# A planner that treats one PSUM bank as one place and keeps TensorE's tiled groups together

## The chip, the core and the metric

The kernel runs on one core of one Trainium2 chip. The metric is the device time of one execution in microseconds (us). Before the change it is 1250.54 us, the median of three runs that lie between 1249.49 and 1253.12 us.

## What is computed

Attention over 8 batches and 8 heads (576 positions, head size 64) with a threshold on the scores, and after it a feed-forward network (FFN) over all 4608 tokens. All data is float32.

```python
scores = scale * np.matmul(q, k.transpose(0, 1, 3, 2))
thresh = np.max(scores, axis=-1, keepdims=True) - tau
scores = np.where(scores >= thresh, scores, -1000000000.0)
attn = np.exp(scores - max); attn = attn / (attn.sum() + 1e-09)
x = np.matmul(attn, v)            # heads side by side: (4608, 512)
h = x @ w_in                      # (4608, 2048)
g = s * np.maximum(h, 0.0) ** 2 + b
out = g @ w_out                   # (4608, 512)
```

## The kernel before

**Attention** is done in 64 visits. A visit takes two heads of one batch and 256 of their queries; every second visit also takes the 64 last queries (the tail). A visit has four tiles of 128 queries by 576 keys, and one more if it has a tail. For a tile TensorE makes the scores in one of the banks `s0`, `s1` (early on also `o`), DVE scales them and takes the minimum (L395), ACT takes the exponential (L406), DVE applies the threshold and sums (L409), and POOL divides (L413). The first eight visits are turned over by TensorE transposes (L423, L425), the later ones by DVE (L446, L448) and by DMA into `er`. Then TensorE makes a visit's value products (L476) into the bank `pv`.

**The FFN** is done in 18 blocks of 256 tokens. A block has 16 steps, one for each 128 columns of `w_in`, so 288 steps in all. A step has twelve matmuls of 256 columns (L599, in f32 parts) into one half of the bank `h`; the halves `h0` and `h1` take turns. ACT reads that half with a Relu (L606) and squares it (L607), `gh` and `gl` are the two parts of the result (L609, L610), and two triples of matmuls of 512 columns (L616) add the step's share to the bank `o`.

**Groups of matmuls that use only a part of the array** (tiled, in the words of the change) are three: the early scores of two heads side by side (L352, tiles of 64 by 128, 24 groups of 4), the tails' scores in quarters (L374, 64 by 64, 28 groups of 4), and the value products (L476, 128 by 64, 64 groups of 10). All the other matmuls (L363, L599, L616 and some early ones) use 128 by 128. The profile counts twice as many instructions for L352, L374 and L476, since each of these f32 matmuls is two there.

**The order of all work** is made by the class `Plan`. Each piece of work is put in with `add`: its engine, a cost, the names it reads (`r`) and writes (`w`), and a rank `at`. From the names `add` works out what must come first. `ordered` is a list scheduler: it takes the engine that is free first and the ready piece of the lowest rank, forwards and backwards in turn (`run`, 8 rounds for each of 18 settings of slack), and `played` rates each order by playing it with random delays; the best one is emitted. Each engine then runs its instructions in the order emitted. The semaphores are not the planner's: a layer below sets them, from the emitted order and the tiles that instructions use, and there the bank `h` is one tile.

Names of the plan that the change touches: a step's matmuls write `h0` or `h1`, and in addition `hs`, which no piece of work reads (`step`); its Relu reads `h0` or `h1`. `sums` (L563) is one product for the bias, also in bank `h`. `pairs` (in `scores`), `last_rows` and `value_products` give the costs of the three tiled groups.

Of the kernel before, what the change touches and what calls it, by code (L numbers as in the profile page):

```python
# [13 lines left out]
AF = mybir.ActivationFunctionType  # L14
# [11 lines left out]
WEIGHTS_AT, WEIGHTS_EACH = 12, 0.8  # L26
FIRST_WEIGHTS = 4
SECOND = 3.5


class Plan:
    HANDOVER, TO_PE = 50, 150
    PASS, OVER = 100, 400
    SPARE = {"DVE": 100, "ACT": 100, "POOL": 100, "SP": 300}
    SHARES = 0.2, 0.4, 0.7
    LATER = 1.0, 1.2, 1.4
# [4 lines left out]
    def __init__(self):  # L41
        self.ops, self.writer, self.readers = [], {}, {}

    def add(self, engine, cost, emit, r=(), w=(), at=0.0, port=False):
        n, deps = len(self.ops), set()
        for k in r:
            if k in self.writer:
                deps.add(self.writer[k])
        for k in w:
            if k in self.writer:  # L50
                deps.add(self.writer[k])
            deps.update(self.readers.pop(k, ()))
            self.writer[k] = n
        for k in r:
            self.readers.setdefault(k, []).append(n)
        deps.discard(n)
        self.ops.append((engine, cost[0], cost[-1], emit, deps, at, port or engine == "POOL"))

    def run(self):
        ops = self.ops  # L60
# [27 lines left out]
        return sum(self.played(order, *slow) for slow in self.SLOW) / len(self.SLOW)  # L88

    def played(self, order, seed, cold, hand=60, to_pe=150, same=40):  # L90
        ops, free, done, port = self.ops, {}, [0.0] * len(self.ops), 0.0
        late = random.Random(seed)
        for _, n in order:
            e, busy, ready, _, deps, _, shared = ops[n]
            t = free.get(e, 0.0)
            for d in deps:
                if ops[d][0] != e:
                    t = max(t, done[d] + (to_pe if e == "PE" else hand))
                elif e != "PE":
                    t = max(t, done[d] + same)  # L100
            if shared and port > t:
                t = port
            tail = ready - busy
            if e in ("DVE", "ACT", "POOL"):
                busy += late.expovariate(1 / self.DELAY)
            elif e == "PE" and t < self.EARLY:
                busy *= cold
            elif e == "SP":
                tail += late.expovariate(1 / self.LANDING)
            free[e] = t + busy  # L110
            if shared:
                port = t + busy
            done[n] = t + busy + tail
        return max(done) / 1000

    def ordered(self, before, after, rank, busy, done, back):
        ops = self.ops
        left = [len(b) for b in before]
        ready = [0.0] * len(ops)
        free, coming, there = {}, {}, {}  # L120
        for n, o in enumerate(ops):
            free[o[0]] = 0.0
            coming.setdefault(o[0], [])
            there.setdefault(o[0], [])
            if not left[n]:
                heapq.heappush(coming[o[0]], (0.0, n))
        order, port = [], 0.0
        for _ in ops:
            best = None
            for e in free:  # L130
                t = free[e]
                while coming[e] and coming[e][0][0] <= t:
                    n = heapq.heappop(coming[e])[1]
                    heapq.heappush(there[e], (rank[n], n))
                if not there[e]:
                    if not coming[e]:
                        continue
                    t = coming[e][0][0]
                if best is None or t < best[0]:
                    best = t, e  # L140
            t, e = best
            while coming[e] and coming[e][0][0] <= t:
                n = heapq.heappop(coming[e])[1]
                heapq.heappush(there[e], (rank[n], n))
            n = heapq.heappop(there[e])[1]
            if ops[n][6] and port > t + self.PASS:
                for at, m in sorted(there[e]):
                    if not ops[m][6] and busy[m] < port - t + self.OVER:
                        there[e].remove((at, m))
                        heapq.heapify(there[e])  # L150
                        heapq.heappush(there[e], (rank[n], n))
                        n = m
                        break
            if ops[n][6]:
                t = max(t, port)
                port = t + busy[n]
            order.append((t, n))
            free[e] = t + busy[n]
            for u in after[n]:
                if ops[u][0] == e == "PE":  # L160
                    late = busy[n]
                else:
                    late = busy[n] + done[u] - busy[u] if back else done[n]
                    p = n if back else u
                    late += 0 if ops[u][0] == e else self.TO_PE if ops[p][0] == "PE" else self.HANDOVER
                ready[u] = max(ready[u], t + late)
                left[u] -= 1
                if not left[u]:
                    heapq.heappush(coming[ops[u][0]], (ready[u], u))
        order.sort()  # L170
        return order
# [3 lines left out]
def tile_attention_ffn(ctx: ExitStack, tc: tile.TileContext, qT, kT, v, tau, w_in, w_out, s, b, out):  # L175
    nc = tc.nc
# [52 lines left out]

    plan = Plan()  # L230

    def pe(cost, fn, r, w, at):
        plan.add("PE", (cost, cost + 170), fn, r, w, at)

    def dve(cost, fn, r, w, at, port=False):
        plan.add("DVE", cost, fn, r, w, at, port)
# [98 lines left out]
    def scores(vs, i, t):  # L335
        n = vs.n
        if t is None:
            def both():
                for hf in range(2):
                    cs = slice(hf * HS, (hf + 1) * HS)  # L340
                    nc.tensor.matmul(flat["s0"][:, S0 + hf * HS:S0 + (hf + 1) * HS], qd[n], kr[:, n, cs], start=True, stop=True)
            pe(970, both, [("k", n)] + vs.kd, ["s0"], i - SCORES_AHEAD)
            return

        ks = [vs.scores_in(i + j, j) for j in range(2)]

        def pairs():
            for hf in range(2):
                cs = slice(hf * HS, (hf + 1) * HS)
                for j in range(2):  # L350
                    r = slice(j * D, (j + 1) * D)
                    nc.tensor.matmul(flat[ks[j]][:, S0 + hf * HS:S0 + (hf + 1) * HS], qr[r, n, t * P:(t + 1) * P], kr[r, n, cs],  # L352
                                     start=True, stop=True)
        pe(980, pairs, vs.kq + ["guard"] + (["h0"] if not i else []), ks, i - SCORES_AHEAD)

    def split_scores(vs, i, j, t):
        sk, qc = f"s{i % 2}", slice(t * P, (t + 1) * P)
# [9 lines left out]
    def last_rows(vs, i, before):  # L367
        sk = f"s{i % 2}"

        def quarters():  # L370
            for r in range(2):
                rows, cs = slice(r * D, (r + 1) * D), slice(r * HS, (r + 1) * HS)
                for j in range(2):
                    nc.tensor.matmul(flat[sk][j * T:(j + 1) * T, S0 + r * HS:S0 + (r + 1) * HS], qr[rows, j, NB:NB + T],  # L374
                                     kr[rows, j, cs], start=True, stop=True)
        cost, r, w = 860, [(x, o) for x in ("rk", "rq") for o in (0, D)], [sk]
        values = None
        if before is not None:
            more, values, r_, w_ = value_products(before)
# [2 lines left out]
        def both():  # L382
            quarters()
            if values:
                values()
        pe(cost, both, r, w, i - SCORES_AHEAD)

    def tile_of(vs, i, j, t):
        sk = vs.scores_in(i, j)
# [78 lines left out]
    def value_products(vs):  # L468
        n, nb = vs.n, vs.nb
        ps = bank["pv"]  # L470

        def products():
            for c in range(5):
                r = slice(0, T if vs.pe and c == NQ else P)
                for j in range(2):
                    nc.tensor.matmul(ps[j * D:(j + 1) * D, 0:32 * nb], vb[r, n, j, c], er[r, n, j, 0:nb, 32 * c:32 * c + 32],  # L476
                                     start=(c == 0), stop=(c == 4))
        return (250 + 66.6 * 4.33 * nb, products,
                [("v", n, x) for x in range(3)] + [("er", n, j, e) for j in range(2) for e in range(nb)], ["pv"])

    def with_v(vs, at, done=False):
        ps = bank["pv"]
        if not done:
            pe(*value_products(vs), at)
        xk = xs[vs.bi, vs.u]
        act((268, 372), lambda: nc.scalar.copy(out=xb[xk][:, vs.pair], in_=ps[:, 0:NB]), ["pv"],
            [("x", xk, vs.pair)], at)
# [73 lines left out]

    def sums(at):
        pe(900, lambda: nc.tensor.matmul(bank["h"], ones.bitcast(F32), bias_t, start=True, stop=True), ["bias", "ones"],  # L563
           ["h0", "h1", "hs"], at)
        act((480, 620), lambda: nc.scalar.mul(out=bias_t, in_=bank["h"], mul=b_t), ["h0", "h1", "b"], ["bias"], at)

    def xhl():
# [4 lines left out]
    class Block:  # L572
# [16 lines left out]
        def step(self, f, at):  # L589
# [9 lines left out]
                        nc.tensor.matmul(ps, w[:, c, :], x[:, c, :], start=(c == 0 and i == 0), stop=(c == NC - 1 and i == 2))  # L599
            if f in (0, NF - 1):  # L600
                for c in range(0, NC, 2):
                    pe(6 * 120.9, lambda c=c: products(range(c, c + 2)), [("xh", c // 2), ("xl", c // 2), (f"w{f}", "i")], [f"h{k}", "hs"], at)
            else:
                pe(3 * NC * 120.9, lambda: products(range(NC)), [(x, c) for x in ("xh", "xl") for c in range(2)] + [(f"w{f}", "i")],
                   [f"h{k}", "hs"], at)
            act((272, 383), lambda: nc.scalar.activation(out=g, in_=ps, func=AF.Relu), [f"h{k}"], [f"g{k}"], at)  # L606
            act((322, 417), lambda: nc.scalar.activation(out=g, in_=g, func=AF.Square), [f"g{k}"], [f"g{k}"], at)  # L607
            eng, do = (nc.vector, dve2) if self.last else (nc.gpsimd, pool)
            act((302, 405), lambda: nc.scalar.copy(out=hi, in_=g), [f"g{k}"], [f"gh{n}"], at)  # L609
# [218 lines left out]
```

## Time and profile before

| | |
|---|---|
| median of three runs | 1250.54 us (1249.49 to 1253.12) |
| the profiled execution | 1250.1 us, of which its span is 1248.3 us |
| TensorE (PE) busy | 1211.1 us, 97% of the span |
| DVE, ACT, POOL busy | 807.1, 767.5, 719.7 us |
| mean granted TensorE clock | 0.987 |

The span is the time from the first to the last instruction of the program; 1.8 us of the profiled execution lie around it. An engine's busy time is the time in which at least one of its instructions runs, and the ends of matmuls are modelled, so successive matmuls overlap in the rows: the distance from one start to the next is what a matmul costs.

### The profile page before, as it was taken

To read this page: it belongs to the slowest core of one execution; us is meant where nothing else is said; L and a number is where in the kernel's file an instruction comes from. 1 tells how busy PE (TensorE), PEld (TensorE's weight loads), DVE (VectorE), ACT (ScalarE), POOL (GpSimd) and SP (SyncE) were. 2 spreads that over 40 slices of the span, in tenths; PEclk is the share of its full clock that TensorE was granted. 3 is DMA by queue.
4 is the path that set the end of the run, shared out by engine and by line. 5 is a ranking of instruction groups with operands and counts; after the bars stand their busy time and mean duration, and the time that the engine had idled before them with its cause. 6 is when DMAs were issued, how large, how long until landed. Compare 5 with 4: busy or idle time off the path is not lost.

```text
span 1248.3 us, 24523 instructions
## 1 busy us (share of the span) xinstructions
PE 1211.1 (97%) x7926; PEld 990.0 (79%) x7926; DVE 807.1 (65%) x2158; ACT 767.5 (61%) x1890; POOL 719.7 (58%) x822
## 2 busy tenths in 40 slices
PE   7789999999999999999999999999999999999998
PEld 5467778787887888788878888888888888887887
DVE  7987876667767676576666677666766666663011
ACT  5777755666666676565665666566656665653443
POOL 3766845576666775575565666557566656652200
PEclk7889999999999999999999999999999999999999
DMA  7950257678768776667666676566766666652000
GB/s 254 282 184 25 53 140 159 153 169 182 173 157 186 170 172 153 150 144 170 136 160 151 150 173 156 143 147 161 162 142 160 161 157 152 158 134 72 1 17 17
DMA packets 259534, 180.66 MB, mean 145 GB/s; under 512 B 83536, under 2 KB 238160, under 8 KB 259408
## 3 DMA queue, kind: packets, MB, share of 16 engines
q1 hardware_dynamic: 259120, 178.98, 59.0%
q8 instruction: 63, 1.03, 0.3%
q14 instruction: 63, 0.52, 0.1%
q10 hardware_dynamic: 288, 0.13, 0.0%
HBM read 87.03 MB, written 9.44 MB: 77 GB/s over the span
## 4 chain that ended last, share of the span: by engine, by line
PE 91%; DVE 4%; ACT 2%; issue 1%; DMA 1%; POOL 1%; SPq 0%; ACTq 0%; DVEq 0%; POOLq 0%
PE h L599 33%; PE o L616 32%; PE pv L476 12%; PE s L363 9%; PE s L352 2%; PE s L374 1%; DVE s L395 1%; ACT g L606 1%; PE pv L425 1%; DVE tr L409 1%; DMA qr<-in_q_dram 0%; DMA tau_t<-in_tau_dram 0%; DVE em L409 0%; DVE k L549 0%; PE o L352 0%
## 5 line engine op out<-in xcount | busy, mean ns | idle before, releaser
L599 PE MATMUL h<-xh,w 128*128 128x256 f32 x2304 | 466.7, 286 | 11.3 <-ACT g L606 11.0
L599 PEld LDWEIGHTS h<-xh,w 128*128 128x128 f32 x2304 | 376.9, 190 | 38.2 <-ACT g L606 23.5
L616 PE MATMUL o<-w,gh 128*128 128x512 f32 x1152 | 366.8, 400 | 0.8 <-DVE em L636 0.6
L599 PE MATMUL h<-xl,w 128*128 128x256 f32 x1152 | 326.1, 283 | 1.5 <-DVE xl L585 1.4
L610 POOL TENSOR_TENSOR gl<-g,gh 128x256 fp32r<-128x256 f32 x272 | 202.8, 747 | 212.0 <-ACT gh L609 188.2
L395 DVE TENSOR_SCALAR_CACHE_REDUCE s<-s,nsc 128x576 f32<-128x576 f32 x283 | 230.5, 819 | 143.1 <-PE s L363 120.8
L413 POOL TENSOR_SCALAR em<-em,st,zero 128x576 f32<-128x576 f32 x270 | 230.1, 853 | 156.7 <-DVE st L412 102.2
L409 DVE SCALAR_TENSOR_TENSOR em<-s,st,em 128x577 f32<-128x577 f32 x268 | 217.5, 812 | 105.8 <-ACT st L404 67.9
L406 ACT ACTIVATE em<-s,st 128x576 f32<-128x576 f32 x268 | 197.8, 738 | 95.9 <-DVE s L395 62.4
L616 PEld LDWEIGHTS o<-w,gh 128*128 128x128 f32 x1152 | 197.0, 189 | 46.3 <-issue 20.4
L616 PE MATMUL o<-w,gl 128*128 128x512 f32 x576 | 225.1, 391 | 0.0
L599 PEld LDWEIGHTS h<-xl,w 128*128 128x128 f32 x1152 | 219.7, 191 | 6.1 <-DVE xl L585 2.0
L446 DVE STREAM_TRANSPOSE tr<-em 128x512 f32<-128x512 f32 x252 | 178.2, 707 | 56.9 <-POOL em L413 47.3
L606 ACT ACTIVATE g<-h 128x256 f32<-128x256 f32 x288 | 109.2, 380 | 171.0 <-PE h L599 160.6
L328 POOL TENSOR_TENSOR k<-kr,k 64x576 fp32r<-64x576 f32 x104 | 148.5, 1428 | 54.1 <-ACT k L327 40.2
L476 PE MATMUL pv<-er,vb 128*64 128x256 f32 (+1 forms) x1280 | 172.8, 416 | 1.6 <-ACT er L434 1.6
L609 ACT CAST gh<-g 128x256 fp32r<-128x256 f32 x288 | 116.2, 405 | 56.6 <-PE o L616 52.9
L363 PE MATMUL s<-k 128*128 128x288 f32 x832 | 144.1, 297 | 0.6 <-POOL k L328 0.6
L363 PEld LDWEIGHTS s<-k 128*128 128x128 f32 x832 | 127.7, 188 | 19.7 <-issue 4.9
L476 PEld LDWEIGHTS pv<-er,vb 128*64 128x64 f32 x1280 | 86.4, 138 | 70.5 <-issue 12.9
L616 PEld LDWEIGHTS o<-w,gl 128*128 128x128 f32 x576 | 108.4, 188 | 24.5
L607 ACT ACTIVATE g<-g 128x256 f32<-128x256 f32 x288 | 119.9, 417 | 5.7
(104 smaller groups left out, 953.3 us busy)
## 6 DMA issues: line engine op xcount, KB each, us to landing
er<-tr SPq DMA_DIRECT2D x448, 160.0 KB, 3.3
kr<-in_k_dram SPq DMA_DIRECT2D x116, 288.0 KB, 4.2
vb<-in_v_dram SPq DMA_DIRECT2D x128, 128.0 KB, 2.8
qr<-in_q_dram SPq DMA_DIRECT2D x56, 160.0 KB, 4.4
er<-tr SPq DMA_DIRECT2D x112, 80.0 KB, 2.5
w<-in_moe_w_in_dram SPq DMA_DIRECT2D x16, 512.0 KB, 6.6
w<-in_moe_w_out_dram SPq DMA_DIRECT2D x16, 512.0 KB, 5.7
out_dram<-oo SPq DMA_DIRECT2D x30, 256.0 KB, 2.6
```

Source lines behind the costliest of these rows:

```text
L328: pool((1500, 1500), lambda: nc.gpsimd.tensor_tensor(out=z()[D:P], in0=kr[D:P, j], in1=z()[D:P].bitcast(F32), op=ALU.subtract), rk + [("z" ...
L363: nc.tensor.matmul(flat[sk][:, S0 + hf * HS:S0 + (hf + 1) * HS], lazy["q"][:, x, j, qc], lazy["k"][:, j, cs], start=(x == 0), stop=(x == 1))
L395: dve((740, 875), lambda: nc.vector.tensor_scalar(out=ps[:, S0:S0 + S], in0=ps[:, S0:S0 + S], scalar1=nsc, scalar2=None, op0=ALU.mult, op1 ...
L406: act((632, 740), lambda: nc.scalar.activation(out=ev, in_=ps[:, S0:S0 + S], func=AF.Exp, bias=st8[:, 0:1], scale=-1.0), [sk, (ks_, 0)], [ ...
L409: dve((742, 830), lambda: nc.vector.scalar_tensor_tensor(out=eb, in0=ps[:, S0:S0 + S + 1], scalar=st8[:, 1:2], in1=eb, op0=ALU.is_le, op1= ...
L413: pool((795, 825), lambda: nc.gpsimd.tensor_scalar(out=ev, in0=ev, scalar1=st8[:, 4:5], scalar2=zero, op0=ALU.mult, op1=ALU.add), [em_k, ( ...
L446: nc.vector.transpose(out=to[:, :, 0:NQ].rearrange("p m c q -> p m (c q)"), in_=ev[:, 0:M].rearrange("p (m r) -> p m r", m=4))
L476: nc.tensor.matmul(ps[j * D:(j + 1) * D, 0:32 * nb], vb[r, n, j, c], er[r, n, j, 0:nb, 32 * c:32 * c + 32], start=(c == 0), stop=(c == 4))
L599: nc.tensor.matmul(ps, w[:, c, :], x[:, c, :], start=(c == 0 and i == 0), stop=(c == NC - 1 and i == 2))
L606: act((272, 383), lambda: nc.scalar.activation(out=g, in_=ps, func=AF.Relu), [f"h{k}"], [f"g{k}"], at)
L610: do((712, 740), lambda: eng.tensor_tensor(out=lo, in0=g, in1=hi.bitcast(F32), op=ALU.subtract), [f"g{k}", f"gh{n}"], [f"gl{n}"], at)
L616: nc.tensor.matmul(bank["o"][:, t, :], a[:, ts_], w, start=(f == 0 and i == 0), stop=(f == NF - 1 and i == 2))
```

## The change

The bank `h` becomes one place in the plan: every step writes both `h0` and `h1`, and its Relu reads both, so that in the plan no step may start before the Relu of the step ahead of it is done. The name `hs` goes. Then the plan knows which PE groups are tiled. When a PE group differs in that from the one before, the plan adds `TURN` = 95 ns, in `ordered` and in `played`; one tiled shape after another counts as no change. When the last PE group was tiled and the next by rank is not, `ordered` looks among the ready groups for a tiled one whose rank is less than `NEAR` = 8000 ns later, and takes that first. The costs of tiled groups become: pairs 1170 instead of 980, quarters 650 instead of 860, value products 170 + 267 for each 32 columns instead of 250 + 288.4. The matmuls and all other instructions stay the same in kind and number.

```diff
+PAIR = 1170
...
+    TURN, NEAR = 95, 8000
...
-        self.ops.append((engine, cost[0], cost[-1], emit, deps, at, port or engine == "POOL"))
+        self.ops.append((engine, cost[0], cost[-1], emit, deps, at, port or engine == "POOL", tiled))
...
     def played(self, order, seed, cold, hand=60, to_pe=150, same=40):
...
             t = free.get(e, 0.0)
+            if e == "PE":
+                t += self.TURN * (tiled != mode)
+                mode = tiled
...
             n = heapq.heappop(there[e])[1]
+            if e == "PE" and mode and not ops[n][7]:
+                for at, m in sorted(there[e]):
+                    if ops[m][7] and at < rank[n] + self.NEAR:
+                        there[e].remove((at, m))
+                        heapq.heapify(there[e])
+                        heapq.heappush(there[e], (rank[n], n))
+                        n = m
+                        break
+            if e == "PE":
+                t += self.TURN * (mode != ops[n][7])
+                mode = ops[n][7]
...
-        pe(980, pairs, vs.kq + ["guard"] + (["h0"] if not i else []), ks, i - SCORES_AHEAD)
+        pe(PAIR, pairs, vs.kq + ["guard"] + (["h0"] if not i else []), ks, i - SCORES_AHEAD, True)
...
-        cost, r, w = 860, [(x, o) for x in ("rk", "rq") for o in (0, D)], [sk]
+        cost, r, w = 650, [(x, o) for x in ("rk", "rq") for o in (0, D)], [sk]
...
-        pe(cost, both, r, w, i - SCORES_AHEAD)
+        pe(cost, both, r, w, i - SCORES_AHEAD, True)
...
-        return (250 + 66.6 * 4.33 * nb, products,
+        return (170 + 267 * nb, products,
...
-            pe(*value_products(vs), at)
+            pe(*value_products(vs), at, True)
...
-           ["h0", "h1", "hs"], at)
+           ["h0", "h1"], at)
...
-                   [f"h{k}", "hs"], at)
-            act((272, 383), lambda: nc.scalar.activation(out=g, in_=ps, func=AF.Relu), [f"h{k}"], [f"g{k}"], at)
+                   ["h0", "h1"], at)
+            act((272, 383), lambda: nc.scalar.activation(out=g, in_=ps, func=AF.Relu), ["h0", "h1"], [f"g{k}"], at)
```

What this does to the emitted order is seen at three places. Lines of the changed kernel are 16 higher: L599 is L615 there, L616 is L632, L363 is L379, L476 is L492, L374 is L390. Left of the arrow stands the tile written, right of it the tiles read; `w4_489` before and `w4_486` in the change are both the weights of step 4 of a block. A line of "..." leaves out a step's other matmuls.

PE, where one block of the FFN begins (its steps 4 to 6). Before:

```order
L363 MATMUL s1_99<-k_1521 128x288 x4
L599 MATMUL h_102<-xh_609,w4_489 128x256
...
L599 MATMUL h_102<-xh_609,w5_562 128x256
...
L599 MATMUL h_102<-xh_609,w6_621 128x256
...
L476 MATMUL pv_101<-er_84,vb_83 64x256 x10
L616 MATMUL o_100<-w0_268,gh2_94 128x512 x2
```

The same place in the change:

```order
L492 MATMUL pv_101<-er_84,vb_83 64x256 x10
L615 MATMUL h_102<-xh_597,w4_486 128x256
...
L379 MATMUL s1_99<-k_1509 128x288 x4
L379 MATMUL s0_98<-k_1509 128x288 x4
L615 MATMUL h_102<-xh_597,w5_545 128x256
...
L632 MATMUL o_100<-w0_248,gh2_94 128x512 x2
```

Before, three steps followed each other; now two groups of scores stand between steps 4 and 5, and second products (L632) after step 5. In the whole program a step followed the step before it with nothing between 39 times before, and does so 2 times now; with one group of scores (L363) alone between them 18 times before, 1 time now.

PE, a tail's quarters and the value products near it. Before, the value products:

```order
L599 MATMUL h_102<-xh_609,w1_299 128x256
L476 MATMUL pv_101<-er_84,vb_83 64x320 x10
L363 MATMUL s0_98<-k_1521 128x288 x4
L616 MATMUL o_100<-w14_1351,gh1_93 128x512 x2
```

and the quarters, some 60 rows later:

```order
L616 MATMUL o_100<-w1_299,gl1_96 128x512
L374 MATMUL s0_98<-kr_81,qr_82 64x288 x4
L616 MATMUL o_100<-w1_299,gh1_93 128x512 x2
```

In the change:

```order
L615 MATMUL h_102<-xh_597,w4_486 128x256
L492 MATMUL pv_101<-er_84,vb_83 64x320 x10
L390 MATMUL s0_98<-kr_81,qr_82 64x288 x4
L615 MATMUL h_102<-xh_597,w5_545 128x256
```

The two tiled groups now follow each other. In the whole program tiled groups stand beside each other 25 times, 11 times before, and PE goes from untiled to tiled work or back 182 times, 210 times before.

PE, the first step of the first block. Before:

```order
L425 MATMUL pv_101<-k_87,em0_77 128x128 x4
L599 MATMUL h_102<-xh_609,w0_268 128x256
...
L599 MATMUL h_102<-xh_609,w0_268 128x256
L423 MATMUL s1_99<-k_87,em1_78 64x128
L425 MATMUL pv_101<-k_87,em1_78 128x128 x4
L352 MATMUL s0_98<-kr_81,qr_82 128x288
...
L425 MATMUL pv_101<-k_87,tr0_79 128x128 x4
L599 MATMUL h_102<-xh_609,w0_268 128x256
```

In the change:

```order
L441 MATMUL pv_101<-k_87,em1_78 128x128 x4
L615 MATMUL h_102<-xh_597,w0_248 128x256
...
L615 MATMUL h_102<-xh_597,w0_248 128x256
L357 MATMUL s0_98<-kr_81,k_87 128x288 x2
L615 MATMUL h_102<-xh_597,w1_309 128x256
```

The first step's two halves stood apart, with transposes and scores between them; now they are one run.

## Rows read from the trace of the kernel before

**Rows 1.** The page: PE's busy time, and the granted clock in 40 slices.

```profile
PE 1211.1 (97%) x7926; PEld 990.0 (79%) x7926; DVE 807.1 (65%) x2158; ACT 767.5 (61%) x1890; POOL 719.7 (58%) x822
...
PEclk7889999999999999999999999999999999999999
```

**Rows 2.** The page: the chain that ended last, share of the span by engine.

```profile
PE 91%; DVE 4%; ACT 2%; issue 1%; DMA 1%; POOL 1%; SPq 0%; ACTq 0%; DVEq 0%; POOLq 0%
```

**Rows 3.** Windows: busy us of each engine by stretch.

```profile
core 0: us, PE busy (x) PEld busy (x) DVE busy (x) ACT busy (x) POOL busy (x), PEclk, DMA share, GB/s
0.00:31.00 31.00, 24.20 (x106) 15.95 (x106) 22.55 (x70) 16.60 (x31) 11.16 (x25) 0.78 0.78 253
31.00:62.00 31.00, 23.39 (x132) 14.57 (x134) 30.57 (x80) 23.36 (x49) 23.46 (x19) 0.84 0.91 287
62.00:94.00 32.00, 27.14 (x166) 19.62 (x165) 25.79 (x65) 22.39 (x53) 20.61 (x19) 0.89 0.58 180
...
562.00:625.00 63.00, 62.05 (x416) 52.24 (x412) 39.67 (x107) 38.34 (x97) 36.84 (x44) 1.00 0.67 156
```

**Rows 4.** PE's waits from 94 us on: who waited for whom, us, times, longest.

```profile
PE h L599 <- ACT g L606: 10.5, 20, 1.0
PE h L563 <- ACT g L606: 1.0, 1, 1.0
```

**Rows 5.** Timeline, PE and ACT: the third of three steps in a row begins.

```profile
1031.70 0.28 PE L599 MATMUL h<-xl,w 128*128 128x256 f32 x1
1031.82 0.28 PE L599 MATMUL h<-xh,w 128*128 128x256 f32 x1
1032.19 0.38 ACT L606 ACTIVATE g<-h 128x256 f32<-128x256 f32 x1 [1.92 <-PE h L599]
...
1032.63 0.38 PE L599 MATMUL h<-xh,w 128*128 128x256 f32 x1 [0.53 <-ACT g L606]
```

**Rows 6.** Timeline of PE: one group of scores between untiled groups.

```profile
331.31 0.69 PE L363 MATMUL s<-k 128*128 128x288 f32 x4
331.83 0.63 PE L616 MATMUL o<-w,gh 128*128 128x512 f32 x2
```

**Rows 7.** Timeline of PE: value products alone between two steps.

```profile
577.42 0.28 PE L599 MATMUL h<-xl,w 128*128 128x256 f32 x1
577.54 0.28 PE L599 MATMUL h<-xh,w 128*128 128x256 f32 x1
577.75 2.38 PE L476 MATMUL pv<-er,vb 128*64 128x256 f32 x20
580.06 0.39 PE L599 MATMUL h<-xh,w 128*128 128x256 f32 x1
580.28 0.28 PE L599 MATMUL h<-xl,w 128*128 128x256 f32 x1
```

**Rows 8.** Timeline of PE: a tail's quarters alone.

```profile
639.62 0.72 PE L374 MATMUL s<-kr,qr 64*64 64x288 f32 x8
640.26 0.39 PE L599 MATMUL h<-xh,w 128*128 128x256 f32 x1
```

**Rows 9.** Timeline of PE: value products and quarters side by side.

```profile
335.96 2.38 PE L476 MATMUL pv<-er,vb 128*64 128x256 f32 x20
338.27 0.72 PE L374 MATMUL s<-kr,qr 64*64 64x288 f32 x8
338.92 0.39 PE L599 MATMUL h<-xh,w 128*128 128x256 f32 x1
339.14 0.28 PE L599 MATMUL h<-xl,w 128*128 128x256 f32 x1
```

**Rows 10.** PE's waits before 94 us.

```profile
PE s L352 <- DVE em L409: 4.9, 3, 4.1
PE s L423 <- POOL tr L413: 2.4, 4, 1.1
...
PE h L599 <- DVE xl L585: 1.4, 1, 1.4
...
PE h L599 <- ACT g L606: 0.5, 1, 0.5
```

**Rows 11.** Waits of the other engines over the whole span, and DMA landing.

```profile
ACT g L606 <- PE h L599: 160.6, 141, 5.0
...
DVE s L395 <- PE s L363: 120.8, 120, 4.6
...
er<-tr SPq DMA_DIRECT2D x448, 160.0 KB, 3.3
```

More of the change, by code (lines that the diff above doesn't have):

```diff
@@ L42, in __init__, with add @@
         self.ops, self.writer, self.readers = [], {}, {}
-    def add(self, engine, cost, emit, r=(), w=(), at=0.0, port=False):
+    def add(self, engine, cost, emit, r=(), w=(), at=0.0, port=False, tiled=False):
         n, deps = len(self.ops), set()
@@ L90, in played @@
     def played(self, order, seed, cold, hand=60, to_pe=150, same=40):
-        ops, free, done, port = self.ops, {}, [0.0] * len(self.ops), 0.0
+        ops, free, done, port, mode = self.ops, {}, [0.0] * len(self.ops), 0.0, False
         late = random.Random(seed)
         for _, n in order:
-            e, busy, ready, _, deps, _, shared = ops[n]
+            e, busy, ready, _, deps, _, shared, tiled = ops[n]
             t = free.get(e, 0.0)
+            if e == "PE":
+                t += self.TURN * (tiled != mode)
+                mode = tiled
             for d in deps:
@@ L126, in ordered @@
                 heapq.heappush(coming[o[0]], (0.0, n))
-        order, port = [], 0.0
+        order, port, mode = [], 0.0, False
         for _ in ops:
@@ L230, in tile_attention_ffn, with pe @@
     plan = Plan()
-    def pe(cost, fn, r, w, at):
-        plan.add("PE", (cost, cost + 170), fn, r, w, at)
+    def pe(cost, fn, r, w, at, tiled=False):
+        plan.add("PE", (cost, cost + 170), fn, r, w, at, tiled=tiled)
     def dve(cost, fn, r, w, at, port=False):
@@ L601, in step @@
                 for c in range(0, NC, 2):
-                    pe(6 * 120.9, lambda c=c: products(range(c, c + 2)), [("xh", c // 2), ("xl", c // 2), (f"w{f}", "i")], [f"h{k}", "hs"], at)
+                    pe(6 * 120.9, lambda c=c: products(range(c, c + 2)), [("xh", c // 2), ("xl", c // 2), (f"w{f}", "i")], ["h0", "h1"], at)
             else:
                 pe(3 * NC * 120.9, lambda: products(range(NC)), [(x, c) for x in ("xh", "xl") for c in range(2)] + [(f"w{f}", "i")],
-                   [f"h{k}", "hs"], at)
-            act((272, 383), lambda: nc.scalar.activation(out=g, in_=ps, func=AF.Relu), [f"h{k}"], [f"g{k}"], at)
+                   ["h0", "h1"], at)
+            act((272, 383), lambda: nc.scalar.activation(out=g, in_=ps, func=AF.Relu), ["h0", "h1"], [f"g{k}"], at)
             act((322, 417), lambda: nc.scalar.activation(out=g, in_=g, func=AF.Square), [f"g{k}"], [f"g{k}"], at)
```

## The prediction

> **What bounds the kernel now.** I read the page first: PE is busy 97% of the span, with the granted clock at full (2.4 GHz) in all but the first slices [rows 1], and the chain of what ended last runs through PE for 91% of the span [rows 2]. So the time is PE's queue of matmuls and the holes in it. Then the windows [rows 3]: from 94 us on a stretch of 63 us has about 1 us without a matmul, while in the first 94 us PE is idle for 31.0 - 24.2, 31.0 - 23.4 and 32.0 - 27.1, together 19.3 us, at a mean clock of 0.78 to 0.89, which means part of the time at 1.2 GHz. There DVE is the full engine: 30.57 of 31 us in the second stretch. Then PE's waits from 94 us on [rows 4]: nearly all of them are steps of the FFN (L599) that wait for ACT's Relu (L606), 20 times, 10.5 us, and once the bias product (L563) with 1.0 us. The timeline shows one of them [rows 5]. The reader is to see two things there. ACT's Relu begins after 1.92 us of idling, right behind the second of two steps in a row, though the first of them was done 1.43 us earlier (twelve matmuls at 0.12 us). And the third step begins when that Relu ends. So a step that is emitted straight behind another one holds up the Relu between them, and the next step then holds up PE. That fits a bank that the semaphores take as one tile, which the old plan did not know: there only `h0` against `h0` and `h1` against `h1` counted.
>
> **The change, part by part.** No instruction goes or comes; what changes is the order, so each term is the holes in PE's queue before and after.
>
> *Steps and their Relu.* The third step in rows 5 starts 0.81 us after the matmul ahead of it instead of 0.12: 0.69 us lost, of which the row calls 0.53 idle, since a matmul of 0.28 us is modelled to run on for 0.16 us after the next one could have started. So a wait costs its idle time and 0.16 us: 10.5 + 20 x 0.16 = 13.7 us for the steps and 1.0 + 0.16 = 1.2 us for the bias product [rows 4], and 0.5 + 0.16 = 0.7 us before 94 us [rows 10]. Together 15.6 us.
>
> What of it stays? By the order of the change a step follows a step directly 2 times instead of 39, which leaves 2 x 0.69 = 1.4 us. One group of scores takes 0.52 us [rows 6], so where it alone stands between two steps 0.69 - 0.52 = 0.17 us is lost: 18 times before, once now, 0.2 us. Fourteen of the 20 waits are direct ones like rows 5 (0.47 to 0.53 us each, 7.2 us); the other six (3.3 us idle, 4.3 us with 0.16 each) come with work between the steps, when ACT is late or the filler is short. I leave half of that, 2.1 us, as the new order puts more work between but does not make ACT faster. The bias product has three triples of second products between the last step and itself now and need not wait. So 15.6 - 1.4 - 0.2 - 2.1 = 11.9 us go. Bounds: nothing of the late ones stays (14.0 us gained), or the stalls come back behind other waits by half (6 us). What fills the gap between two steps is work that has to be done anyway, above all second products (L616) and scores, so it costs nothing; if it were not ready, PE would wait there instead, see the rivals.
>
> *Tiled groups side by side.* Alone between two steps, value products start 0.21 us after the last matmul ahead instead of 0.12, take 2.31 us until the next group starts, and that group's second matmul comes 0.22 us after its first instead of 0.12 [rows 7]. So a lone group pays 0.09 us at its entry and 0.10 us in the group behind it. The quarters alone take 0.64 us to the next group's start [rows 8]. Side by side the value products take 2.31 us and the quarters 0.65 us, the same as alone [rows 9]; what falls away is one 0.10 us behind the first group and one 0.09 us ahead of the second. That is 0.19 us a pair, and the order has 25 such pairs instead of 11: 14 x 0.19 = 2.7 us gained.
>
> The plan counts a tiled group behind one of another tiled shape as no change at all. Rows 7 and 9 speak against it: the 2.31 us of the value products are no shorter when the next group is tiled too (128 by 64 against 64 by 64). If that change were free, I would expect at least another 0.09 us a pair, 14 x 0.28 = 3.9 us. The sum goes by the rows, 2.7 us; the bounds are 0 and 3.9 us.
>
> The Trainium skill, in TensorEngine Tiling (Array Packing), Tiling Modes, Key Properties, says that a change of the tiling mode, and not only of the tile, drains the engine. By that rule the value products and the quarters beside them, two modes, would still drain between them, and the gain is that of the rows, not the 3.9 us that the plan's reckoning suggests; the trace agrees with it here, with 2.31 us in both places.
>
> *The first 94 us.* The first step's halves now run together, where the second one had waited 1.4 us for DVE's `xl` [rows 10]; early scores cost the plan 1170 instead of 980 ns, which shifts a few scores and transposes among each other. DVE has the same work to do before the first step can begin, and it is the full engine there [rows 3], so I take zero, with bounds of 4 us to either side: about what the early waits hold that an order could make or remove (without the first of 4.1 us: 0.8 + 2.4 + 1.4 = 4.6 us, rows 10).
>
> *The costs.* New costs of tiled groups in the plan move work only through the order; beyond the terms above I give them nothing. The end of the program has the same steps; the two direct crossings that are left lie there, and are in the first term. POOL and the DMA queue get the same instructions in another order; neither is named among PE's waits from 94 us on with more than 0.6 us.
>
> **The sum.** 11.9 + 2.7 = 14.6 us less than the profiled execution's 1250.1 us (span 1248.3 and 1.8 us around it): 1235.5 us. The median of the runs, 1250.54, is 0.4 us above that execution, so I expect a median of **1235.9 us**. With the bounds: at best 14.0 + 3.9 + 4 = 21.9 us gained, 1228.6; at worst 6 + 0 - 4 = 2 us, 1248.5.
>
> **The rivals.**
>
> *The wait moves to the scores.* With a Relu between all steps PE has to be fed from the scores' banks just when they are asked for, and a group of scores (208 with L363) needs DVE to have finished the threshold (L409) of the tile that used that bank. Against it: DVE itself sat idle 120 times, 120.8 us, for PE's scores [rows 11], and PE waits for L409 only early on. For it: two groups of scores now stand side by side as filler at a block's start, and the second needs a bank freed by then. At 0.05 us on average over 208 groups it gives 10.4 us back: 1246. I give 1243 to 1247 a chance of 0.12.
>
> *A tiled group is pulled forward before its data is there.* This is the one that ends slower. `ordered` takes a tiled group up to 8 us ahead of its rank; for value products that is the DMA into `er`, which takes 3.3 us to land [rows 11]. Everything behind waits with it in PE's queue. Fourteen groups at the full 3.3 us are 46 us, 1282; the gain of 14.6 us is used up at 1.04 us for each. Against it: only groups that are ready by the plan are taken, the plan reckons 3.35 us for that DMA, and no wait for `er` stands among PE's waits from 94 us on. Likeliest outcome if it happens: a dozen waits of 1.5 us, 18 us, 1254. Chance 0.05 for anything slower by more than 0.3%.
>
> *Nothing gained.* The plan is picked from 144 orders by a play with random delays, and a new rule reshuffles all of them; the early stretch could lose what the steps gain (4 us there, and waits for ACT that are only shifted: 6 us left). That is 1247 to 1254, chance 0.07.
>
> *More than the sum.* If the early stretch gains 4 us and ACT's late Relus vanish as well, 1229; chance 0.08.
>
> *The forecast* itself, 1230 to 1243, gets the rest, 0.68.
>
> **The numbers.** The range leaves out about half of "more than the sum" below and the two worst cases above: 1230 to 1245 us. A difference under 0.3%, 3.75 us, can't be told from none. Faster than 1246.8 by forecast, more than the sum, and the scores' case: 0.68 + 0.08 + 0.12 = 0.88; within 0.3% 0.07; slower 0.05.
>
> **What would show it.** In the profile of the changed kernel PE's waits from 94 us on should have L599 <- ACT L606 down from 10.5 us to some 2 to 4 us and the bias product's wait gone; the idle time of ACT's Relu for PE should hold few waits as long as a whole step. PE's busy share should rise to 98%. Value products next to quarters should show 2.31 and 0.65 us and no wait for `er`. The windows to 94 us should hold 74 to 78 us of PE work, as before (74.7). Wrong it would be if L363, L374 or L476 appear among PE's waits with several us, or if the first 94 us lose more than 4 us of PE's work.

## The result, and the profile after

| | before | after |
|---|---|---|
| median of four runs, us | 1250.01 (1247.5 to 1253.12) | **1229.22** (1227.29 to 1229.58) |
| profiled execution, us | 1250.1 | 1229.16 |
| its span, us | 1248.3 | 1227.2 |

The ratio is 0.9829, with a 95% interval of 0.9805 to 0.9854. The forecast was 1235.9 us with a range of 1230 to 1245: right in sign and in kind, but the time is 0.8 us below the range. The gain is 20.8 us where 14.6 were reckoned. The mean granted clock is 0.987 in both profiled executions, so the clock does not make the difference.

The page of the changed kernel, PE's busy time and the granted clock; it answers to [rows 1].

```profile
PE 1198.6 (98%) x7926; PEld 987.3 (80%) x7926; DVE 798.6 (65%) x2158; ACT 765.1 (62%) x1890; POOL 718.3 (59%) x822
...
PEclk7899999999999999999999999999999999999999
```

PE's waits from 94 us on, which answer to [rows 4]. L615 and L622 are the step and its Relu.

```profile
PE h L615 <- ACT g L622: 1.4, 3, 0.5
PE o L632 <- DVE em L652: 0.6, 1, 0.6
PE s L439 <- DVE s L411: 0.2, 1, 0.2
```

Twenty waits of 10.5 us have become 3 of 1.4, and the bias product (L579 here) waits no more. The timeline of PE at the place of the first order excerpt: value products (L492) and two groups of scores (L379) between steps, and every step starts on time (0.12 us behind the last matmul, or behind the work between).

```profile
1009.34 0.28 PE L615 MATMUL h<-xh,w 128*128 128x256 f32 x1
1009.55 2.38 PE L492 MATMUL pv<-er,vb 128*64 128x256 f32 x20
1011.86 0.38 PE L615 MATMUL h<-xh,w 128*128 128x256 f32 x1
1012.08 0.28 PE L615 MATMUL h<-xl,w 128*128 128x256 f32 x1
...
1013.28 0.28 PE L615 MATMUL h<-xh,w 128*128 128x256 f32 x1
1013.40 1.23 PE L379 MATMUL s<-k 128*128 128x288 f32 x8
1014.47 0.28 PE L615 MATMUL h<-xh,w 128*128 128x256 f32 x1
1014.58 0.28 PE L615 MATMUL h<-xl,w 128*128 128x256 f32 x1
```

Value products and quarters side by side, which answer to [rows 9]: the value products take 2.31 us to the quarters (209.51 - 207.20) and the quarters 0.64 us to the next group (210.15 - 209.51), as before and as alone.

```profile
207.20 2.38 PE L492 MATMUL pv<-er,vb 128*64 128x256 f32 x20
209.51 0.72 PE L390 MATMUL s<-kr,qr 64*64 64x288 f32 x8
210.15 0.39 PE L615 MATMUL h<-xh,w 128*128 128x256 f32 x1
210.38 0.28 PE L615 MATMUL h<-xl,w 128*128 128x256 f32 x1
```

The windows to 94 us, which answer to [rows 3]: 24.5 + 21.8 + 25.8 = 72.1 us of PE work in 394 matmuls, against 74.7 in 404 before. The beginning has become a little worse, not better.

```profile
0.00:31.00 31.00, 24.52 (x106) 15.94 (x106) 20.64 (x67) 16.41 (x32) 10.08 (x23) 0.72 0.75 249
31.00:62.00 31.00, 21.76 (x122) 12.93 (x122) 27.47 (x72) 21.16 (x46) 23.91 (x20) 0.83 0.83 269
62.00:94.00 32.00, 25.78 (x166) 17.94 (x167) 28.96 (x72) 24.38 (x55) 23.87 (x19) 0.95 0.58 190
```

### The profile page after: what moved, and what is told of

Its sections match the earlier page's. It is cut to its first block, busy times and chain, and to the rows that moved or that the text cites. A ratio compares the mean times of both kernels' runs of the same rounds, so it can differ in the third digit from the quotient of the medians.

```text
span 1227.2 us, 24552 instructions
## 1 busy us (share of the span) xinstructions
PE 1198.6 (98%) x7926; PEld 987.3 (80%) x7926; DVE 798.6 (65%) x2158; ACT 765.1 (62%) x1890; POOL 718.3 (59%) x822
## 4 chain that ended last, share of the span: by engine, by line
PE 93%; DMA 2%; DVE 2%; ACT 1%; issue 1%; POOL 1%; SPq 0%; ACTq 0%; DVEq 0%; POOLq 0%
PE h L615 34%; PE o L632 32%; PE pv L492 13%; PE s L379 9%; PE s L368 2%; PE s L390 1%; PE pv L441 1%; DVE s L411 1%; DMA tau_t<-in_tau_dram 1%; DMA vb<-in_v_dram 1%; DMA qr<-in_q_dram 0%; DMA w<-in_moe_w_out_dram 0%; PE s L357 0%; PE s L439 0%; ACT em L422 0%
## 5 line engine op out<-in xcount | busy, mean ns | idle before, releaser
L615 PE MATMUL h<-xh,w 128*128 128x256 f32 x2304 | 467.1, 284 | 2.5 <-ACT g L622 2.5
L615 PEld LDWEIGHTS h<-xh,w 128*128 128x128 f32 x2304 | 377.5, 190 | 29.4 <-issue 11.2
L632 PE MATMUL o<-w,gh 128*128 128x512 f32 x1152 | 365.5, 399 | 0.6 <-DVE em L652 0.6
L615 PE MATMUL h<-xl,w 128*128 128x256 f32 x1152 | 325.2, 282 | 0.6 <-DVE xl L601 0.6
L632 PEld LDWEIGHTS o<-w,gh 128*128 128x128 f32 x1152 | 196.6, 189 | 37.3 <-issue 11.9
L632 PE MATMUL o<-w,gl 128*128 128x512 f32 x576 | 224.7, 390 | 0.6 <-POOL gl L626 0.6
L615 PEld LDWEIGHTS h<-xl,w 128*128 128x128 f32 x1152 | 219.0, 190 | 6.4 <-DVE xl L601 0.8
L622 ACT ACTIVATE g<-h 128x256 f32<-128x256 f32 x288 | 110.2, 383 | 172.4 <-PE h L615 151.5
L492 PE MATMUL pv<-er,vb 128*64 128x256 f32 (+1 forms) x1280 | 174.2, 418 | 3.4 <-ACT er L450 3.4
L344 POOL TENSOR_TENSOR k<-kr,k 64x576 fp32r<-64x576 f32 x104 | 148.5, 1429 | 45.6 <-ACT k L343 31.5
L492 PEld LDWEIGHTS pv<-er,vb 128*64 128x64 f32 x1280 | 86.9, 139 | 74.0 <-issue 14.8
L379 PE MATMUL s<-k 128*128 128x288 f32 x832 | 142.8, 296 | 0.2
L379 PEld LDWEIGHTS s<-k 128*128 128x128 f32 x832 | 126.9, 188 | 15.2 <-issue 2.1
L632 PEld LDWEIGHTS o<-w,gl 128*128 128x128 f32 x576 | 108.2, 188 | 25.8 <-POOL gl L626 1.3
```

The lines of the kernel that those rows point to most:

```text
L344: pool((1500, 1500), lambda: nc.gpsimd.tensor_tensor(out=z()[D:P], in0=kr[D:P, j], in1=z()[D:P].bitcast(F32), op=ALU.subtract), rk + [("z" ...
L379: nc.tensor.matmul(flat[sk][:, S0 + hf * HS:S0 + (hf + 1) * HS], lazy["q"][:, x, j, qc], lazy["k"][:, j, cs], start=(x == 0), stop=(x == 1))
L632: nc.tensor.matmul(bank["o"][:, t, :], a[:, ts_], w, start=(f == 0 and i == 0), stop=(f == NF - 1 and i == 2))
```

## Where PE's time goes: one account for all runs

PE's matmuls are the same 7926 in every run, so the start of the last one is the undisturbed time of the others and the losses; the span ends 4.7 to 5.9 us behind that start. For each trace I took the distance from each matmul's start to the next one's, less what the same matmul takes in an undisturbed run (0.12 us for L599, 0.23 for L616, 0.13 for L363, and so on), and sorted what is left by what comes next. That is a count over all rows of the timeline. The undisturbed time is 1142.2 us in all of them; before, the last matmul starts at 1142.2 + 101.4 = 1243.6 us. From 94 us on the losses are sorted, and up to there they stand in one column, which also holds what the lower clock costs there. "Steps" are late starts of L599 and slow second matmuls of a step, where no tiled group stands ahead of it; "tiled" is all that is lost at the entry and exit of tiled groups, inside them, and in the second matmul behind them. "Rest" can be below zero, since undisturbed times are rounded up, and the columns add up to the sum within 0.3 us.

| run | steps | bias product | tiled | rest | first 94 us | all lost | median us |
|---|---|---|---|---|---|---|---|
| before | 19.3 | 1.2 | 34.2 | 0.8 | 46.0 | 101.4 | 1250.0 |
| **after** | 2.6 | 0 | 30.8 | -0.2 | 47.3 | 80.3 | 1229.2 |
| e1_bank_only | 2.5 | 0 | 34.8 | 4.1 | 45.4 | 86.7 | 1235.2 |
| e2_tiled_only | 26.6 | 0 | 34.6 | 2.7 | 41.4 | 105.4 | 1254.2 |
| e3_costs_only | 23.1 | 0 | 36.3 | 8.6 | 41.6 | 109.5 | 1259.8 |
| e4_relu_ahead | 37.4 | 1.2 | 37.1 | 1.8 | 47.8 | 125.1 | 1274.9 |
| e5_no_pull | 5.2 | 0 | 34.4 | 0.3 | 46.2 | 86.0 | 1233.9 |
| e6_seeds | 4.1 | 0 | 32.5 | 1.8 | 41.8 | 80.0 | 1230.0 |
| e7_bank_seeds | 3.6 | 0.8 | 33.6 | 2.5 | 44.0 | 84.2 | 1232.8 |
| e8_near_turn | 4.3 | 0 | 29.2 | 3.4 | 46.2 | 82.8 | 1232.0 |
| e9_direct | 12.7 | 0 | 30.8 | 0.2 | 45.9 | 89.3 | 1239.3 |
| e10_shapes | 2.9 | 0 | 30.5 | 2.2 | 42.3 | 77.8 | 1227.1 |
| e11_more_play | 4.4 | 0 | 30.6 | 1.1 | 45.6 | 81.4 | 1230.4 |
| e12_near | 5.8 | 0 | 30.1 | 0.7 | 46.5 | 82.9 | 1231.6 |

Before to after, 21.1 us: steps 16.7, bias product 1.2, tiled groups 3.4, the rest 1.0, and 1.3 given back in the first 94 us. Of the 3.4 us at tiled groups 2.7 are the neighbouring pairs: from 94 us on 94 runs of tiled groups have become 80, and the 14 entries and 14 second matmuls that fell away are 0.19 us a pair. Most of the remainder is the Relu once more: before, two steps behind a tiled group waited for it, 0.69 and 0.21 us, and stand in the column "tiled". One of them:

```profile
118.38 0.39 PE L599 MATMUL h<-xh,w 128*128 128x256 f32 x1 [0.62 <-ACT g L606]
```

What the change leaves is lost in the first 94 us for the most part, 47.3 of 80.3 us.

## The experiments

Theory A: the gain is the holes behind the Relu, which come from a bank that the semaphores treat as one, and a smaller part is the pairs of tiled groups. The rivals are told in the expectations. A ratio compares a run with the kernel before as measured beside it: 1248.1 us in e1 to e4, 1250.8 in e5 to e8, 1248.3 in e9 to e12. Medians of different groups can therefore differ by 2 to 3 us without a cause in the kernel; where it matters, the account of the traces decides.

**Only the bank as one place in the plan of before.**

```diff
-                   [f"h{k}", "hs"], at)
+                   ["h0", "h1"], at)
-... func=AF.Relu), [f"h{k}"], [f"g{k}"], at)
+... func=AF.Relu), ["h0", "h1"], [f"g{k}"], at)
```

> The kernel before with the bank as one place in the plan alone; costs and tiled rules as before. Its order has 2 direct crossings of steps instead of 39, and 11 neighbouring pairs of tiled groups as before. Theory A (the holes in PE's queue behind the Relu are the gain): the trace of before loses 15.0 us from 94 us on in starts of L599 that come late, and another 0.10 us in the second matmul behind some 40 of them, 1.2 us at L563 and 0.7 us early; some 3 us of that stay, so about 17 to 18 us go: 1232 to 1234 us. Rival B (most of it comes from the tiled groups and the new costs): 1243 to 1248. Rival C (any new order of this planner lands elsewhere by chance): anywhere from 1228 to 1252, with waits for the Relu as many as before.

1235.19 us (1234.84 to 1240.33), ratio 0.9898 (0.9871 to 0.9925). The step losses are those of the whole change, 2.5 us. It ends a little above the range of theory A because transposes come later (some 3 us of the 4.1 in the rest).

PE's waits for the Relu from 94 us on, in e1_bank_only:

```profile
PE h L599 <- ACT g L606: 1.0, 2, 0.5
```

**Only costs and tiled rules, the bank as two places.**

```diff
-                   ["h0", "h1"], at)
+                   [f"h{k}", "hs"], at)
-... func=AF.Relu), ["h0", "h1"], [f"g{k}"], at)
+... func=AF.Relu), [f"h{k}"], [f"g{k}"], at)
```

> The changed kernel with the bank as two places in the plan again, as before; costs, the reckoned changes of mode and the pulling of tiled groups stay. Its order has 45 direct crossings and 27 neighbouring pairs. Theory A: 16 pairs more at 0.19 to 0.25 us each are 3 to 4 us gained, the waits for the Relu are as many as before or somewhat more (70 Relus stand behind the next step in the order, 60 before): 1246 to 1251 us. Rival B: 1230 to 1238. Rival C: anywhere.

1254.15 us (1249.14 to 1255.62), ratio 1.0032 (1.0013 to 1.0052): no gain, rather a loss, and beyond what theory A allowed. The steps lose 7.3 us more than before, and the 16 pairs more save nothing on balance, since two tiled groups now wait for DVE (the first 15.2 us below are the Relu's, the two others are tiled groups, lines L368 and L390).

```profile
PE h L615 <- ACT g L622: 15.2, 26, 1.4
PE s L368 <- DVE tr L425: 1.9, 1, 1.9
PE s L390 <- DVE em L425: 1.6, 1, 1.6
```

**Only the new costs.**

```diff
-        pe(980, pairs, ...
+        pe(1170, pairs, ...
-        cost, r, w = 860, ...
+        cost, r, w = 650, ...
-        return (250 + 66.6 * 4.33 * nb, products,
+        return (170 + 267 * nb, products,
```

> The kernel before with the three new costs of tiled groups alone (1170, 650, 170 + 267). Its order has 41 direct crossings and 8 neighbouring pairs. Theory A: no gain, 1249 to 1253 us. Rival B, if the costs carry it: under 1242. Rival C: anywhere; this run also shows how far chance alone moves the time.

1259.84 us (1259.41 to 1260.54), ratio 1.0086 (1.0067 to 1.0105): slower than expected. Steps lose 3.8 us more, late second products (L616) 5.0 us more (7.1 against 2.1, in the rest). Of the 3.8 us 1.1 are no waits: behind a hole of 2.9 us at 136 us the granted clock is 1.2 GHz from 139.2 to 142.6 us, and the matmuls of one step come 0.21 us apart instead of 0.12 (the window below; its clock share is 0.50). So as long as the plan has the bank wrong, another order can land 10 us off; that much of rival C holds. Whether the new costs or chance made this order worse is open: no run plays the old bank with other seeds. The three orders planned with the bank wrong take 1250 to 1260 us, the nine planned with it right (e9, mended by hand, left out) 1227 to 1235.

```profile
139.20:142.60 3.40, 3.40 (x18) 3.38 (x17) 2.99 (x9) 2.70 (x6) 1.93 (x2) 0.50 0.02 5
```

**The old order, with each Relu ahead of the next step.**

```diff
+        for units, relu in self.relus:
+            late = [n for n in units if seq.index(n) < seq.index(relu)]
+            for n in late:
+                seq.remove(n)
+            at = seq.index(relu) + 1
+            seq[at:at] = late
```

> The kernel before, plan and all, with the emitted order mended by hand: the 63 steps that stood ahead of the Relu of the step before them are moved to right behind that Relu; everything else stays. 28 direct crossings and 16 with one group of scores between stay in PE's order. Theory A with the bank as one tile for the semaphores: now each of these waits for its Relu, 28 x 0.79 + 16 x 0.27 = 26 us and 4 us for late ones, against 19 us lost in the kernel before, so slower: 1257 to 1263 us, with 25 or more waits of L599 for L606. Rival D (the halves of the bank are tracked apart, and a Relu is late only because ACT is): then a Relu earlier in the order can only help, 1240 to 1250 us, with fewer waits.

1274.94 us (1273.83 to 1276.73), ratio 1.0208 (1.0187 to 1.0229). Rival D falls: a Relu emitted in time makes the kernel slower by 2%, since then nearly every direct crossing waits. The number of waits was right (42; 28 and 16 were counted), the size was not: the steps lose 37.4 us where 30 were reckoned, and 5 us more than before are lost at tiled groups and in the first 94 us. The timeline shows one step behind another (L610 and L621 are the step and its Relu there); the Relu starts as soon as the step ahead is done, and the next step, in the other half, waits for its end.

```profile
1172.97 0.28 PE L610 MATMUL h<-xh,w 128*128 128x256 f32 x1
1173.35 0.38 ACT L621 ACTIVATE g<-h 128x256 f32<-128x256 f32 x1 [3.58 <-PE h L610]
1173.79 0.38 PE L610 MATMUL h<-xh,w 128*128 128x256 f32 x1 [0.53 <-ACT g L621]
1174.01 0.28 PE L610 MATMUL h<-xl,w 128*128 128x256 f32 x1
```

The two halves lie in one bank. The Trainium skill, in PSUM — Partial Sum Buffer, PSUM bank collisions raise a hardware error, says that two engines must not be at the same bank and partitions at once, at whatever address; by that the wait could not be taken away with finer semaphores. No run here tried that.

**No pulling of tiled groups.**

```diff
-    TURN, NEAR = 95, 8000
+    TURN, NEAR = 95, -1
```

> The changed kernel without the pulling of ready tiled groups (NEAR = -1): the bank as one place, the new costs and the reckoned change of mode stay. Its order has 11 neighbouring pairs, as the kernel before, and 3 direct crossings. Theory A with the pairs worth 0.19 to 0.25 us each: 14 pairs fewer than the changed kernel, 3 to 4 us slower than it, 1232 to 1234 us. Rival E (the 6 us between bank only and the whole change are not the pairs but another order of the rest by chance): any time between 1226 and 1240.

1233.86 us (1232.49 to 1234.72), ratio 0.9864 (0.9834 to 0.9894). Tiled groups lose 34.4 us, near the 34.2 of before, against 30.8 with the pairs: 3.6 us. But 1.5 of them are one group of quarters that waited for DVE (1.4 us idle, below), so the 14 pairs are worth some 2.1 us, 0.15 us each. The steps lose 2.6 us more, which I put down to chance of the order; other orders with the bank right lose 2.5 to 5.8 us there.

```profile
PE s L390 <- DVE em L425: 1.4, 1, 1.4
```

**The changed kernel, and bank only, with other seeds in the planner's play.**

```diff
-    SLOW = (1, 1.3), (2, 1.5), (3, 1.7), (4, 1.5)
+    SLOW = (11, 1.3), (12, 1.5), (13, 1.7), (14, 1.5)
```

> The changed kernel with other random delays in the play that picks the order (seeds 11 to 14); 24 neighbouring pairs, 4 direct crossings. It shows what chance in the picked order is worth. Theory A: the holes behind the Relu and the tiled groups are as in the changed kernel, and what differs are the first 125 us and late transposes, 3 us to either side: 1226 to 1233. Rival E or C: over 1235.

> Bank only, as in the first of these runs (1235.2 us there), with other random delays in the play (seeds 11 to 14); 9 neighbouring pairs, 3 direct crossings. Theory A: waits of steps for the Relu 2 to 4 us in all as there, the time 1231 to 1239 us. Rival C: anywhere, waits as many as in the kernel before.

1229.95 us (1229.13 to 1230.51) and 1232.78 us (1231.38 to 1233.42). With the bank right other seeds move the spans by 0.1 us (the whole change) and 2.5 us (bank only). The first 94 us differ most (41.8 against 47.3). Twice bank only gives 1235.2 and 1232.8, twice the whole change 1229.2 and 1230.0: tiled rules and costs are worth 4.4 us on top of the bank by the medians, 5.3 by the account; about half of it stands in the column "tiled", the other half in the rest, where no run tells a cause from chance.

**What a direct crossing costs by itself.** The second products between two steps are moved behind the second of them, at every other of the last 28 steps.

```diff
+        for k in range(259, 287, 2):
+            first, last = seq.index(self.steps[k - 1][-1]), seq.index(self.steps[k][0])
+            for at, n in enumerate(seq[first + 1:last]):
+                if ops[n][0] == "PE":
+                    key[n] = seq.index(self.steps[k][-1]) + 0.001 * (at + 1)
```

> The changed kernel with the emitted order mended by hand in the last 28 steps: at every second one the second products between it and the step before are moved behind it. 14 direct crossings instead of 2; the plan is the same. It measures what one wait for the Relu costs where nothing else is near. By the prediction's price (0.69 us a wait) 12 more are 8.3 us. By the price with the slower second matmul behind a wait (0.69 + 0.10) they are 9.5 us: 1238 to 1239 us; from 155 us before the end on the trace should show 12 second matmuls of a step at 0.22 us. Rival D (halves tracked apart): no loss, 1229.

1239.25 us (1238.27 to 1240.06): 10.0 us above the changed kernel's median, and 9.0 in the spans (1236.2 against 1227.2). The timeline, one of the 14 (L633 and L642 are the step and its Relu there):

```profile
1137.53 0.28 PE L633 MATMUL h<-xl,w 128*128 128x256 f32 x1
1137.65 0.28 PE L633 MATMUL h<-xh,w 128*128 128x256 f32 x1
1138.03 0.38 ACT L642 ACTIVATE g<-h 128x256 f32<-128x256 f32 x1 [1.26 <-PE h L633]
1138.47 0.38 PE L633 MATMUL h<-xh,w 128*128 128x256 f32 x1 [0.53 <-ACT g L642]
1138.69 0.28 PE L633 MATMUL h<-xl,w 128*128 128x256 f32 x1
```

1138.47 - 1137.65 - 0.12 = 0.70 us late, and then 1138.69 - 1138.47 = 0.22 us to the second matmul instead of 0.12. By the account the 12 more crossings cost 8.0 us in late starts and 1.3 us in second matmuls, 0.78 us each (eight of the 14 start 0.69 us late, six 0.63): the price with the second matmul, not the prediction's 0.69.

**Versions that might beat it.** Pulled from farther off with a dearer change of mode; tiled shapes kept apart in the plan; a wider choice of orders; pulled from farther off alone.

```diff
e8_near_turn:
-    TURN, NEAR = 95, 8000
+    TURN, NEAR = 170, 20000
e10_shapes:
-        pe(PAIR, pairs, ..., i - SCORES_AHEAD, True)
+        pe(PAIR, pairs, ..., i - SCORES_AHEAD, 1)
... quarters 2, value products 3
e11_more_play:
-ROUNDS = 8
+ROUNDS = 16
-    SLOW = (1, 1.3), (2, 1.5), (3, 1.7), (4, 1.5)
+    SLOW = tuple((n, c) for n in range(1, 5) for c in (1.3, 1.5, 1.7))
e12_near:
-    TURN, NEAR = 95, 8000
+    TURN, NEAR = 95, 20000
```

> The changed kernel with NEAR = 20000 and TURN = 170: tiled groups are pulled from farther off, and a change of mode is reckoned at about what the rows show for a lone group, half at each end. Its order has 34 neighbouring pairs instead of 25 and 3 direct crossings. Theory A: 9 pairs at 0.25 us, 2 us less than the changed kernel: 1226 to 1228 us, if chance in the rest (3 us) doesn't hide it. Rival F (pulled from so far off, value products come before their data): waits of L492 or L390 in the profile and 1232 or more.

> The changed kernel in which the plan reckons a change between two tiled shapes too (three shapes kept apart, 95 ns each). 23 neighbouring pairs, 3 direct crossings. Theory A: the matmuls cost what they cost, whatever the plan believes of shapes, so as the changed kernel within chance: 1226 to 1233 us.

> The changed kernel with twice the rounds of the planner and twelve plays for each order instead of four. 23 neighbouring pairs, 5 direct crossings. Theory A: if a wider choice finds a better first 125 us, up to 4 us less, 1225; if not, the same within chance, 1226 to 1233.

> The changed kernel with NEAR = 20000 alone (TURN as it is). 31 neighbouring pairs, 4 direct crossings. Theory A: 6 pairs at 0.2 us, 1.2 us less than the changed kernel, within chance: 1225 to 1232 us. Rival F (pulled too early): waits of L492 or L390, and slower than 1232.

1231.99 (1231.56 to 1233.17), 1227.05 (1225.68 to 1229.01), 1230.41 (1230.3 to 1233.17) and 1231.64 us (1230.84 to 1233.56). The ratios to the kernel before are 0.9852 (0.9822 to 0.9882), 0.9828 (0.98 to 0.9856), 0.9861 (0.9828 to 0.9894) and 0.9866 (0.9839 to 0.9894), against the change's 0.9829: none can be told from it as a better one. e8 missed what was expected of it, 1226 to 1228. With 34 pairs e8 does lose 1.6 us less at tiled groups (29.2), as expected, but 1.7 us more at steps and 3.6 in the rest; rival F, tiled groups that wait for their data, does not appear in e8: no L492 or L390 is among its waits from 94 us on, and the losses at tiled groups fell. In e12 one group of value products waits 0.9 us for ACT. Wider choice (e11) loses 45.6 us in the first 94, which is within the spread of the table.

## Why the prediction missed

- **The cause was right.** Steps that wait for the Relu were the main hole from 94 us on that the change closes, the bank being one for the semaphores (e4), and the plan's knowledge of it removes it: 19.3 us of step losses become 2.5 with that alone (e1), 2.6 in the change.
- **The step that failed is "Steps and their Relu": a term of 11.9 us that measured 17.3** (16.7 for steps from 94 us on, 1.2 for the bias product, less 0.6 us that the early waits grew). It was mis-sized in three places. First the price of a wait: "a wait costs its idle time and 0.16 us" leaves out the slower second matmul, 0.10 us more, though rows 5 end one row short of showing it; e9 measures 0.78 us for a direct wait. From 94 us on there were 42 such second matmuls before and 7 after, 3.7 us. Second the number: the waits view counts only those in which PE sat idle beyond the modelled end, 20; by the starts there are 31 late ones, 14.9 us instead of 13.7. Third what stays: 3.7 us were kept back, 1.9 us of late starts stayed; with more work between the steps the late Relus went too, where I had left half of them. Against that, 0.7 us of waits before 94 us were to go, and 0.6 us came: 11.9 + 3.7 + 1.2 + 1.8 - 1.3 = 17.3. The two steps behind tiled groups would come on top (33 late starts and 15.8 us with them); the account has their 0.9 us under "tiled".

A wait that the view does not show, in the trace of the kernel before: the Relu ends at 1188.61, the step starts at 1188.66 with no idle time against it, and its second matmul still comes 0.22 us later.

```profile
1187.96 0.63 PE L616 MATMUL o<-w,gh 128*128 128x512 f32 x2
1188.22 0.39 ACT L606 ACTIVATE g<-h 128x256 f32<-128x256 f32 x1 [1.26 <-PE h L599]
1188.43 0.39 PE L616 MATMUL o<-w,gl 128*128 128x512 f32 x1
...
1188.66 0.39 PE L599 MATMUL h<-xh,w 128*128 128x256 f32 x1
1188.88 0.28 PE L599 MATMUL h<-xl,w 128*128 128x256 f32 x1
```

- **Tiled groups side by side: right.** 2.7 us forecast, and 2.7 measured at the pairs, 0.19 us each, out of 3.4 in the column (0.15 each against e5). Value products take 2.31 us to the next start whether a tiled or an untiled group comes, so the 0.28 us a pair that the plan's reckoning suggested is not seen; telling the plan of the three shapes (e10) changes nothing that can be told.
- **The first 94 us: taken as zero, 1.3 us lost** (0.6 of it the early waits for the Relu, counted above), within the bounds. The sign that was named, 74 to 78 us of PE work there, was missed with 72.1. It goes with the order: 41.4 to 47.8 us are lost there in these 14 orders, and no run tells why.
- **The range was too narrow on the fast side.** At best 21.9 us gained stood in the text, and 20.8 came; the range stopped at 1230. That the median lies at the 1229 of "more than the sum" is luck in part: the late Relus did vanish, but the early stretch lost 1.3 us and did not gain 4.
- **The rivals.** Scores did not become the wait: L379 is not among PE's waits from 94 us on, and neither is L492, so value products did not come before their data there. Both were argued from waits in the trace of before, and rightly. In the first 94 us L492 does wait longer for `er`, 3.4 us against 1.6.

## What to carry to other kernels

Tell a planner what the semaphores enforce: two halves of a bank are two buffers in the program and one in the order, and a plan that believes in two makes holes in the engine that is full. Price a wait of PE from start to start, over the next two matmuls, and count late starts rather than rows of idle time, since modelled ends hide up to 0.16 us of each wait, and the slower second matmul behind it shows only as a distance between rows. When a planner's order is part of what is measured, run it with other seeds before believing in differences of 2 to 3 us.

## What was not expected of the hardware

Behind every one of the 31 late starts of a step, the second matmul of 256 columns comes 0.22 us after the first instead of 0.12, the same as behind a tiled group [rows 7]. The weight loads go with it (PEld is the load of a matmul's weights). Within a step a load starts 0.12 us ahead of its matmul; at 1032.63 us the load of the step that waited starts together with its matmul, and the next load 0.10 us later.

```profile
1031.70 0.19 PEld L599 LDWEIGHTS h<-xh,w 128*128 128x128 f32 x1
1031.82 0.28 PE L599 MATMUL h<-xh,w 128*128 128x256 f32 x1
...
1032.63 0.19 PEld L599 LDWEIGHTS h<-xh,w 128*128 128x128 f32 x1 [0.74 <-ACT g L606]
1032.63 0.38 PE L599 MATMUL h<-xh,w 128*128 128x256 f32 x1 [0.53 <-ACT g L606]
1032.73 0.19 PEld L599 LDWEIGHTS h<-xl,w 128*128 128x128 f32 x1
1032.85 0.28 PE L599 MATMUL h<-xl,w 128*128 128x256 f32 x1
```

All 283 steps that begin from 94 us on in the kernel before fall into two sorts. In 67 the second matmul comes 0.20 us or more behind the first, and the first one's load starts at most 0.03 us ahead of it; in the other 216 it comes after 0.11 to 0.16 us, and the load starts 0.06 to 0.23 us ahead. So the slow second matmul goes with a late weight load there without exception, also in the step at 1188.66, which starts almost on time. That the late load is the reason was not tried by a change of its own.
